# A new hand-stored order of 2278 work pieces in a fused attention and gated-MLP kernel

## Chip, cores, metric

The kernel runs on one core of one Trainium2 chip. The metric is device time in microseconds (us) of one execution, as the median of several runs. Times "in the trace" come from one profiled execution and count from its first instruction.

## What is computed

```python
B, H, S, D = 8, 8, 576, 64
def sm_attn(qq, kk, vv):                       # softmax attention
    s = scale * np.matmul(qq, kk.transpose(0, 1, 3, 2))
    s = s - np.max(s, axis=-1, keepdims=True)
    a = np.exp(s)
    a = a / (np.sum(a, axis=-1, keepdims=True) + 1e-09)
    return np.matmul(a, vv)
...
out_d = sm_attn(q_d, k_d, v_d)                 # q, k, v averaged over 4 positions
out_up = np.repeat(out_d, 4, axis=2)
mask = np.abs(pos[:, None] - pos[None, :]) < 4 # and attention over 7 neighbours
...
x = (out_up + out_local)                       # 8 batches of 576 x 512
h = gelu(x @ w_in)                             # 512 -> 1024, halves u and v
v_n = (v - mu) / np.sqrt(var + 1e-06) * g_ln
v_s = np.einsum('ts,bsd->btd', w_sg, v_n) + b_sg[None, :, None]
return x + (u * v_s) @ w_out
```

## The kernel before, in words

The kernel is written as small **pieces** (`Task`, line 55): a name, the engines that can do it, and a function that emits its instructions. There are 2278. A piece of attention carries the number g = 0 to 31 of its pair of heads (four pairs to a batch), a piece of the MLP the batch and a number, as `s7.1`. The program is the pieces in the order of the string `ORDER` (line 89); `place` (line 66) walks it, gives each piece its buffers from three pools (8 PSUM banks, 10 and 38 SBUF buffers), and the loop at the kernel's end (line 1157 on) emits each piece. A word such as `qs0/V` puts the piece on VectorE; without a letter it goes to the first engine in its table. So the string sets the order on every engine's queue, on the DMA queue of SP, and, where a piece has a choice, its engine. Waits between engines follow from the data; each engine works through its queue strictly in that order.

For each pair g:

- Loads on SP: `lq`, `lk` (q and k), `lv` (v for the pooled attention), `lw` (v in windows). All go through one helper (line 236), which lets at most six be under way.
- `qs`, `ks` (line 481 on DVE as one reduction; lines 484 and 485 on POOL as two additions): sums over four positions, for the pooled scores.
- `S` (L507, L514) local scores and `Y` (L535) pooled scores on PE; from the fifth pair on they are one piece `YS`.
- `mx`, `my` row maxima on DVE; `ea`, `eb`, `ec` exponentials on ACT; `rc`, `np`, `nq` normalization.
- `T`, `U`, `t` (L616, L625) transposes on PE; `pa`, `pb`, `pc`, `pe` (L244) copies out of PSUM.
- `D` (L677, L693): probabilities times v on PE. For the first four pairs `D` reads unsummed v and has four times the pooled matmuls.
- `oe`, `od`, `xa`, `xb` (L700): the pair's x; `xh`, `xl` (L712): x split into two parts for the exact-enough products on PE.

For each batch: `v` (L801; in the first batch cut into `vk` for each pair) and `u` products; `vg`, `vb`, `vp`, `vn`, `vh`, `vl` (L887) the layer norm and its split; `s` (L896) the product over positions; `sa`, `sm` (L943, L949) bias and gate; `ga` to `gd`, `gh`, `gl` (L990, L1002) combinations and splits; `o` (L1019), `oa` (L1026), and the stores `os`. The weights are loaded as 64-bit words and converted on the chip, once, at the start: `wz`, `wy`, `wr` with their `wq`, `wu`, `wb`, `wt`, `wh`, `wl` (L350 to L373), and `wq0` to `wq4` for the square matrix (L441).

At two places (`WARM`) PE gets matmuls on zeros ahead of a piece: 28 ahead of `S0`, 20 ahead of `S3`.

Of the kernel before, what the change touches and what calls it, by code (L numbers as in the profile page):

```python
# [94 lines left out]
wuy3 wqy3/A nq2/P U2 t2 xa0 xb0 ks5/P wby1 xh0/A YS4 pb2/A pc2/A nq3/P np3/P xl0/P t3 lw1 wuy1 wty1 pe2/A whz0/A
wlz0/P ma4 my4 ny4/A mb4 U3 wz2 wqz2/A lv2 ec4 T3 pa3/A pb3/V pc3/A pe3/A D1 mx4 wby3 wty3 lq5 qs5/V wbz2 nx4/A why1/A
wly1/P oe1/A od1 lw3 wuz2 YS5 ma5 vk3.0 xa1 xb1 vk1.0 lv3 ea4 mb5 vk0.0 wtz2 mx5 eb4 whz2/A re4/A my5 ny5/V lw2 nx5/A
D2 why3/A xh1/V ec5 vk2.0 wty2 xl1/V vk3.1 lv4 vs4 D3 wlz2/V rc4 nq4/P wr2 why2/A wly2/P oe2/V od2 xa2 xb2 wq0 wz1 lq6
eb5 ea5 xh2/A wq1 np4/V vk2.1 oe3/V od3 xa3 vk0.1 xb3 xh3/V xl3/P whq0/A U4 xl2/V wly3/V whq1/A wqz1/A t4 re5/A T4
pa4/A vk1.1 pb4/A pc4/A wur2 wbz1 wuz1 xc2 xc0 xc1 vk0.2 wtz1 wqr2/V wbr2 rc5 nq5/P lv5 lk6 np5/P ks6/V pe4/A vk2.2  # L100
v0.2 vg0.2 wq2 wq3 whq3/A wlq3/P vk1.2 v0.0 vg0.0 qs6/V vb0.2/V v0.1 vg0.1 lw4 D4 YS6 whq2/A whz1/A wlz1/P my6 ny6/A
lq8 ma6 mb6 ec6 mx6 nx6/A oe4/V wlq1/V lk7 vs5 wlq0/P vk3.2 od4 xa4 T5 vk4.0 eb6 vk4.1 ks7/V pa5/V vb0.0/V vp0.0 lq7
qs7/V vk4.2 ea6 re6/A u0.4 rc6 qs8/V u0.2 xb4 t5 u0.5 ua0.4 xc3 v0.4 ua0.5 ua0.2 U5 va0.4/A pb5/V pc5/A vb0.1/V u0.3
nq6/P np6/P lk8 v0.3 ks8/V pe5/A lw5 D5 lv6 ua0.3 vp0.2 vg0.3 vn0.0/V b wr1 lw7 wqr1/V vn0.2/A vj0.4 wq4 YS7 oe5/V
vb0.3/A T6 vh0.0/A vg0.4 my7 ny7/A wr0 u0.6 lw6 od5 ma7 mb7 vh0.2/A pa6/V xa5 vp0.1 vn0.1/A ec7 vb0.4/V vh0.1/A ua0.6
u0.1 xb5 mx7 t6 U6 pb6/V pc6/V pe6/V vl0.2/V wlq2/P vs6 u0.0 u0.7 vl0.1/V whq4/A ua0.0 D6 YS8 vp0.3 wur0 ua0.1 nx7/V
vp0.4 vn0.4/V vn0.3/V vh0.4/A ua0.7 wlq4/V ea7 vl0.0/V eb7 vh0.3/V vl0.3/V lv7 vs7 wr3 vl0.4/V s0.1 s0.5 ma8 mb8 re7/A
wbr1 mx8 my8 ny8/A rc7 oe6/A s0.0 ec8 xh5/A nq7/V s0.2 t7 np7/P U7 od6 xa6 sa0.1 sm0.1/P xl5/V sa0.0 wqr0/A lq9 lk9
ks9/V xb6 wur1 wqr3/A lk10 nx8/A T7 s0.3 qs9/V pa7/A pb7/A pc7/A pe7/A lq10 sm0.0/P sa0.2 D7 YS9 eb8 lv8 lk11 qs10/V
sa0.3 sm0.3/V sa0.5 wtr1 ea8 s0.4 sm0.2/P gh0.1/A re8/A vs8 s0.6 xh6/A my9 ny9/A ec9 rc8 np8/V T8 xl6/P oe7/A lw8  # L110
nq8/V U8 sa0.4 ma9 mb9 ks10/V mx9 pa8/A pb8/A pc8/A whr1/A t8 od7 pe8/V sm0.5/P xa7 s0.7 sa0.7 wtr2 ks11/V xh4/A
sm0.4/P sa0.6 xl4/P xb7 xh7/V xl7/P nx9/A eb9 ea9 D8 oe8/A YS10 lq12 v1.1 lv9 gh0.2/A whr2/A ma10 re9/A mb10 xc5 mx10
u1.4 v1.2 xc6 my10 od8 xa8 rc9 xb8 sm0.7/P np9/V T9 gh0.0/A vs9 wlr1/P xc7 v1.0 wbr0 wtr0 ny10/A ua1.4 ec10 vg1.2 wur3
u1.5 nq9/P U9 t9 vg1.0 pa9/A vg1.1 wbr3 wtr3 ua1.5 xc4 gl0.2/V lq11 qs11/V lw9 pb9/A pc9/V v1.3 pe9/V lk12 gl0.0/P
ks12/V vb1.0/A D9 whr0/A YS11 whr3/A lv10 vb1.1/V wlr3/V lw10 vp1.0 nx10/A v1.4 gl0.1/V vn1.0/A vh1.0/A sm0.6/V
gh0.3/A wlr2/V zf3/V my11 vg1.3 vb1.3/A vb1.2/A vp1.2 eb10 gl0.3/V o0.6 ma11 wlr0/V ny11/V vn1.2/A oe9/V mb11 mx11
nx11/A ea11 o0.7 od9 oa0.6 oa0.7 o0.4 oa0.4 vl1.0/P xa9 va1.4/V o0.0 vs10 lk13 qs12/V u1.3 zf0/P vp1.3 vp1.1 oa0.0
ks13/V o0.1 oa0.1 ea10 re10/A rc10 ec11 eb11 o0.3 vj1.4 re11/A vn1.3/A vh1.3/A o0.5 zf1/P zs1/V np10/V rc11 T10 nq11/V
pa10/V oa0.5 vg1.4 o0.2 zs3/V oa0.2 vn1.1/A nq10/V u1.1 vh1.1/V zs2/V U10 pb10/V ua1.1 pc10/A t10 pe10/A xb9 xh8/A
u1.0 ua1.0 vl1.3/V vh1.2/V np11/V vb1.4/A vp1.4 zh2/A zh1/A oa0.3 ua1.3 vn1.4/A D10 oe10/V YS12 my12 lq13 ny12/A ma12  # L120
mb12 ec12 u1.7 vh1.4/A u1.2 od10 os0.2 vl1.1/P xa10 xb10 mx12 ua1.2 lv11 os0.0 nx12/A zf2/P u1.6 vl1.2/P qs13/V U11
vl1.4/V zh3/A T11 pa11/V pb11/A t11 ua1.7 s1.1 sa1.1 os0.3 xh10/A ua1.6 pc11/V pe11/V lw11 ea12 eb12 re12/A s1.0 xl8/V
zs4/V vs11 D11 lv12 YS13 oe11/V s1.2 od11 lk15 sa1.0 my13 vs12 ny13/A lw12 xa11 lq14 qs14/V sm1.0/P ec13 os0.1 s1.4
rc12 nq12/P zl1/V sa1.2 ma13 mb13 mx13 nx13/V s1.3 s1.5 xh9/A xl9/V sm1.2/V np12/V T12 sm1.1/P sa1.3 lk14 sm1.3/P xb11
# [1097 lines left out]
```

## Time and profile before

| | us |
|---|---|
| runs | 564.33, 564.66, 565.92; median 564.66 |
| profiled execution: span from the first to the last instruction | 563.4 |
| median less span | 1.26 |
| PE busy | 547.7 (97%) |
| DVE busy | 445.5 (79%) |
| ACT busy | 392.7 (70%) |
| POOL busy | 331.9 (59%) |
| DMA | 62.73 MB, 111 GB/s on average |

The page states the span of the profiled execution; the time around it is put at the 1.26 us between that span and the median of the runs. PE, DVE, ACT and POOL are the matrix, vector, scalar and GpSimd engines, SP the one whose queue issues the DMAs. "Busy" of PE contains the matmuls on zeros. A matmul's row can start before the one ahead of it has ended, so the length of a row is more than its share of the engine's time.

### The profile page before, as it was taken

How to read it: one execution, taken by the hardware profiler on the slowest of the kernel's cores; microseconds unless marked ns; L12 is line 12 of the kernel's file. 1: busy time of each engine (PE TensorE's matmuls, PEld its weight loads, DVE VectorE, ACT ScalarE, POOL GpSimd, SP SyncE). 2: the span in 40 equal slices, each digit the busy share in tenths (PEclk: the TensorE clock that was granted, in tenths of full speed). 3: DMA queues.
4: the chain of work that ended last, by engine and by line, in shares of the span. 5: the costliest groups of instructions: out<-in, count | busy, mean ns of one | idle time of the engine just before them, and what ended most of it. 6: DMA issues, size and time to landing. Idle time of an engine off the chain costs nothing.

```text
span 563.4 us, 17546 instructions
## 1 busy us (share of the span) xinstructions
PE 547.7 (97%) x6948; PEld 511.2 (91%) x6948; DVE 445.5 (79%) x939; ACT 392.7 (70%) x1320; POOL 331.9 (59%) x447
## 2 busy tenths in 40 slices
...
GB/s 283 273 227 341 203 93 172 95 57 23 181 126 103 34 163 121 100 2 107 153 157 46 46 186 85 136 1 103 92 109 119 66 78 129 71 1 1 0 1 169
DMA packets 31041, 62.73 MB, mean 111 GB/s; under 512 B 3696, under 2 KB 4720, under 8 KB 30960
## 3 DMA queue, kind: packets, MB, share of 16 engines
...
q14 instruction: 26, 0.21, 0.1%
HBM read 52.17 MB, written 9.44 MB: 109 GB/s over the span
## 4 chain that ended last, share of the span: by engine, by line
PE 76%; ACT 6%; DVE 5%; POOL 4%; issue 2%; DMA 0%; DVEq 0%; ACTq 0%; POOLq 0%
PE ps L896 36%; PE ps L801 14%; PE ps L1019 12%; PE ps L677 3%; PE ps L693 2%; PE ps L616 2%; PE ps L625 2%; PE ps L535 2%; PE ps L514 2%; ACT X L574 2%; ACT R L244 1%; DVE R L990 1%; POOL pairs L498 1%; ACT pd L596 1%; POOL wsg_l L441 0%
## 5 line engine op out<-in xcount | busy, mean ns | idle before, releaser
L896 PE MATMUL ps<-wsg_h,R 128*128 128x288 f32 x576 | 122.5, 300 | 0.2 <-DVE R L887 0.2
L896 PE MATMUL ps<-X,weight_z 128*128 128x288 f32 x512 | 109.5, 297 | 0.3 <-ACT R L924 0.3
L801 PE MATMUL ps<-weight_y,X 128*128 128x512 f32 x320 | 98.3, 400 | 0.1
L574 ACT ACTIVATE X<-X,nb 128x64 f32<-128x64 f32 x280 | 93.5, 339 | 5.1 <-DVE nb L553 4.7
L896 PEld LDWEIGHTS ps<-wsg_h,R 128*128 128x128 f32 x576 | 93.9, 188 | 1.3 <-DVE R L887 0.4
L896 PE MATMUL ps<-wsg_l,R 128*128 128x288 f32 x320 | 92.6, 295 | 0.0
L896 PEld LDWEIGHTS ps<-X,weight_z 128*128 128x128 f32 x512 | 84.2, 188 | 1.2 <-ACT R L924 0.6
L896 PE MATMUL ps<-R,weight_z 128*128 128x288 f32 x256 | 75.4, 295 | 0.0
L801 PEld LDWEIGHTS ps<-weight_y,X 128*128 128x128 f32 x320 | 57.6, 188 | 11.9 <-POOL X L244 0.3
L1026 DVE TENSOR_TENSOR R<-ps,R 128x288 f32<-128x288 f32 x98 | 42.1, 448 | 25.2 <-PE ps L1019 24.9
L896 PEld LDWEIGHTS ps<-wsg_l,R 128*128 128x128 f32 x320 | 60.3, 189 | 0.0
L244 ACT COPY R<-ps 128x116 f32<-128x116 f32 (+3 forms) x80 | 27.2, 381 | 40.9 <-DVE R L244 11.9
L574 ACT ACTIVATION_READ_ACCUMULATOR X<-X,nb 128x1 f32 x280 | 53.3, 190 | 0.0
L1019 PE MATMUL ps<-R,weight_r 128*128 128x288 f32 x336 | 51.0, 298 | 0.3 <-DVE R L700 0.3
L244 ACT CAST R<-R 128x576 fp32r<-128x576 f32 (+2 forms) x61 | 39.1, 647 | 17.4 <-POOL R L990 10.5
L801 PE MATMUL ps<-weight_y,R 128*128 128x512 f32 x128 | 50.4, 394 | 0.0
L498 POOL TENSOR_TENSOR pairs<-R 112x256 f32<-112x256 f32 x56 | 45.0, 804 | 6.1 <-DMA R<-in_v_dram 6.0
L896 PEld LDWEIGHTS ps<-R,weight_z 128*128 128x128 f32 x256 | 48.2, 188 | 0.3
L943 DVE SCALAR_TENSOR_TENSOR vs<-ps,g_sb,b_sb 128x288 f32<-128x288 f32 x64 | 32.3, 512 | 20.1 <-PE ps L896 16.9
L1019 PEld LDWEIGHTS ps<-R,weight_r 128*128 128x128 f32 x336 | 46.6, 188 | 1.4 <-issue 0.5
L1002 POOL TENSOR_TENSOR R<-R,R 128x576 fp32r<-128x576 f32 x21 | 32.1, 1534 | 23.4 <-ACT R L244 9.8
L949 POOL TENSOR_TENSOR R<-R,vs 128x288 f32<-128x288 f32 x27 | 24.5, 909 | 35.4 <-DVE vs L943 29.4
...
## 6 DMA issues: line engine op xcount, KB each, us to landing
...
X<-in_vw_dram SPq DMA_DIRECT2D x32, 320.0 KB, 4.4
R<-in_kT_dram SPq DMA_DIRECT2D x32, 293.0 KB, 3.9
R<-in_qT_dram SPq DMA_DIRECT2D x32, 293.0 KB, 3.8
...
weight_z<-in_w_in_dram SPq DMA_DIRECT2D x4, 512.0 KB, 5.8
weight_y<-in_w_in_dram SPq DMA_DIRECT2D x4, 512.0 KB, 6.0
weight_r<-in_w_out_dram SPq DMA_DIRECT2D x4, 512.0 KB, 5.8
```

What stands on the lines that cost most here:

```text
L244: (nc.scalar.copy if e == "A" else ENG[e].tensor_copy)(**kw)
L498: ENG[e].tensor_tensor(out=pairs, in0=v[:, 0:2], in1=v[:, 2:4], op=ALU.add)
L514: nc.tensor.matmul(out=sp[i][os, c * KB:(c + 1) * KB], lhsT=q[hs, t * QB:t * QB + KB], rhs=k[hs, t * QB:t * QB + KB], start=not early, sto ...
L574: nc.scalar.activation(out=st["ms"][:, t, :], in_=src, func=AF.Exp, bias=st["nb"][:, t:t + 1], scale=scale, accum_out=sums[par][:, t:t + 1])
L677: nc.tensor.matmul(out=out, lhsT=lhsT, rhs=pdt[ks, probs, h * QC:(h + 1) * QC], start=first, stop=last)
L801: nc.tensor.matmul(out=acc, lhsT=r32(l), rhs=r32(weights[f"y{k}"][:, 0, w]), start=(i == 0 and ks[0] == 0), stop=(i == len(ops) - 1 and ks ...
L896: nc.tensor.matmul(out=acc[:, 0:HALF], lhsT=r32(l), rhs=r32(r), start=(first and n == 0), stop=(last and n == len(ops) - 1))
L943: nc.vector.scalar_tensor_tensor(out=vsb[i], in0=at["ps", "m", b, "s", i][:, 0:HALF], scalar=g_sb[:, i // 2:i // 2 + 1], in1=b_sb[:, half( ...
L949: ENG[e].tensor_tensor(out=gate(i), in0=gate(i), in1=vsb[i], op=ALU.mult)
L1002: ENG[e].tensor_tensor(out=r32(gl[m]), in0=us[raws[m]], in1=gh[m], op=ALU.subtract)
L1019: nc.tensor.matmul(out=bank(j, c), lhsT=r32(l), rhs=r32(r), start=first and i == 0, stop=i == len(ops) - 1, skip_group_check=not first)
L1026: nc.vector.tensor_tensor(out=x, in0=bank(j, c), in1=x, op=ALU.add)
```

## The change

Only the string `ORDER` is another; the pieces, their functions, the pools and everything else are the same. Of the string's 2278 words nearly all stand at another place, and 369 pieces go to another engine: for instance 25 of the 40 `vl` are on POOL where 17 were, and 32 of the 40 `vb` on ACT where 25 were. The first lines of the table:

```diff
 ORDER = """
-wz3 wuz3 lk0 ks0/P wqz3/V wbz3 wy0 wqy0/V wby0 lq0 lk2 lk1 wtz3 whz3/A wlz3/P S0 lq1 qs0/V Y0 mx0 ia0 lq3 my0 ks1/P
-wuy0 qs1/P ib0 ea0 small wty0 S1 mx1 ks2/V lq2 qs2/P ia1 es0 ny0/A ec0 re0/A ib1 ea1 Y1 lk3 my1 rc0 S2 mx2 why0/A ia2
...
+wz3 wqz3/V wuz3 lq0 qs0/P wbz3 wtz3 whz3 lk0 ks0 S0 lk1 ks1 mx0 lq2 Y0 wy0 wqy0 qs2/P wlz3 lq1 my0 S1 ia0 ny0/V ib0 wby0
+qs1/P lk5 lk2 wuy0 mx1 wty0 ea0 es0 ec0 re0 ia1 lq3 why0 Y1 qs3/P my1 rc0 nq0 wy2 wqy2 wuy2 lk3 wz0 ny1 S2 S3 mx2 ib1
...
```

Three places are shown as the built programs have them. In the rows of the change every line number below the table is smaller by 10, since its table is ten lines shorter.

The first loads in SP's queue, before (`weight_z3`, `weight_y0` are `wz3`, `wy0`; the `R` buffers are `lk0`, `lq0`, `lk2`, `lk1`, `lq1`):

```order
L236 DMA weight_z3_154<-in_w_in_dram 128x2x512
L236 DMA R0_157<-in_kT_dram 128x586
L236 DMA weight_y0_167<-in_w_in_dram 128x1024
L236 DMA R3_174<-in_qT_dram 128x586
L236 DMA R4_176<-in_kT_dram 128x586
L236 DMA R5_178<-in_kT_dram 128x586
L236 DMA R6_237<-in_qT_dram 128x586
```

And in the change (`wz3`, `lq0`, `lk0`, `lk1`, `lq2`, `wy0`, `lq1`):

```order
L226 DMA weight_z3_154<-in_w_in_dram 128x2x512
L226 DMA R0_158<-in_qT_dram 128x586
L226 DMA R2_170<-in_kT_dram 128x586
L226 DMA R3_226<-in_kT_dram 128x586
L226 DMA R4_231<-in_qT_dram 128x586
L226 DMA weight_y0_243<-in_w_in_dram 128x1024
L226 DMA R5_250<-in_qT_dram 128x586
```

The load of `weight_y0` moved from the third place to the sixth, so q and k of the first pair are now second and third.

DVE's queue from the first weight to the first row maximum, before (L352 to L358 convert a weight; L481 is `qs0`; L544 is `mx0`):

```order
L352 TENSOR_SCALAR weight_z3_154<-weight_z3_154 128x512
L308 MEMSET mask_sb_70 128x3
L309 MEMSET mask_sb_70 128x7
L356 TENSOR_SCALAR ps0_163<-weight_z3_154 128x512
L358 SCALAR_TENSOR_TENSOR R1_164<-weight_z3_154,ps0_163 128x512
L352 TENSOR_SCALAR weight_y0_167<-weight_y0_167 128x512
L356 TENSOR_SCALAR ps1_170<-weight_y0_167 128x512
L358 SCALAR_TENSOR_TENSOR R2_171<-weight_y0_167,ps1_170 128x512
L481 TENSOR_REDUCE qd0_80<-R3_174 128x144
L544 TENSOR_REDUCE stats0_84<-ps2_213 128x4
```

And in the change (L471 twice: `ks0`, `ks1`; L534: `mx0`):

```order
L342 TENSOR_SCALAR weight_z3_154<-weight_z3_154 128x512
L298 MEMSET mask_sb_70 128x3
L299 MEMSET mask_sb_70 128x7
L346 TENSOR_SCALAR ps0_163<-weight_z3_154 128x512
L348 SCALAR_TENSOR_TENSOR R1_164<-weight_z3_154,ps0_163 128x512
L471 TENSOR_REDUCE kd0_88<-R2_170 128x144
L471 TENSOR_REDUCE kd1_89<-R3_226 128x144
L534 TENSOR_REDUCE stats0_84<-ps1_202 128x4
```

The three operations on `weight_y0` went behind the first row maximum (one of them to ACT); `qs0` went to POOL, and `ks0`, `ks1` came from POOL to DVE.

POOL's queue in the last batch, around the splits `vl` that the product `s7.1` waits for, before (L887 is `vl7.3`; L853 to L855 are `vp`; L1002 is `gl6.5`):

```order
L854 TENSOR_TENSOR rs_104<-rs_104,nhalf 128x1
L855 TENSOR_SCALAR nm_109<-mv_101,rs_104 128x1
L887 TENSOR_TENSOR R_8486<-R_8440,R_8483 128x512
L853 TENSOR_SCALAR rs_105<-rs_105 64x1
L854 TENSOR_TENSOR rs_105<-rs_105,nhalf 64x1
L855 TENSOR_SCALAR nm_110<-mv_102,rs_105 64x1
L1002 TENSOR_TENSOR R_8550<-R_7730,R_8548 128x576
```

And in the change (L877 is `vl`: `vl7.4`, then `vl7.1`, `vl7.0`, `vl7.3`; L992 is `gl6.4`, and last `gl6.6`):

```order
L992 TENSOR_TENSOR R_8481<-R_8320,R_8322 128x576
L877 TENSOR_TENSOR R_8483<-R_8369,R_8483 64x512
L843 TENSOR_SCALAR rs_104<-rs_104 128x1
L844 TENSOR_TENSOR rs_104<-rs_104,nhalf 128x1
L845 TENSOR_SCALAR nm_109<-mv_101,rs_104 128x1
L877 TENSOR_TENSOR R_8525<-R_8371,R_8465 128x512
L877 TENSOR_TENSOR R_8539<-R_8277,R_8520 128x512
L877 TENSOR_TENSOR R_8580<-R_8487,R_8535 128x512
L992 TENSOR_TENSOR R_8621<-R_8405,R_8619 128x576
```

Before, one of the batch's five `vl` was on POOL and four on DVE; now four are on POOL, three of them in a row.

## Rows read from the trace of the kernel before

**Rows 1.** Stretch, length, busy PE, PEld, DVE, ACT, POOL; PE clock, DMA share, GB/s.
```profile
0.00:70.50 70.50, 59.43 (x1078) 49.86 (x1079) 60.66 (x142) 53.09 (x182) 55.55 (x72) 0.95 0.82 265
14.10:28.20 14.10, 12.36 (x237) 10.51 (x232) 13.94 (x32) 11.91 (x44) 12.26 (x15) 0.86 0.86 273
70.50:549.90 479.40, 477.97 (x5796) 451.21 (x5795) 377.01 (x781) 338.60 (x1138) 272.96 (x375) 1.00 0.28 87
549.90:563.40 13.50, 10.33 (x79) 10.10 (x77) 7.81 (x19) 1.01 (x2) 3.41 (x2) 1.00 0.49 176
```

**Rows 2.** What PE waited for: us in total, times, longest.
```profile
PE ps L514 <- DMA R<-in_qT_dram: 2.3, 1, 2.3
PE ps L693 <- issue: 2.2, 1, 2.2
PE ps L535 <- DVE qd L481: 2.1, 2, 1.4
```

**Rows 3.** Timeline of PE: start us, length us, line, operation [idle before <-releaser].
```profile
8.68 0.93 PE L514 MATMUL ps<-R,R 64*64 64x64 f32 x40 [2.30 <-DMA R<-in_qT_dram]
11.00 1.18 PE L535 MATMUL ps<-kd,qd 64*64 64x144 f32 x16 [1.38 <-DVE qd L481]
...
25.51 2.93 PE L677 MATMUL ps<-R,R 48*64 48x144 f32 x56
...
33.47 1.72 PE L677 MATMUL ps<-R,R 48*64 48x144 f32 x59
...
41.10 1.71 PE L677 MATMUL ps<-R,R 48*64 48x144 f32 x60
...
45.06 1.71 PE L677 MATMUL ps<-R,R 48*64 48x144 f32 x60
...
49.47 0.45 PE L693 MATMUL ps<-R,X 64*64 64x58 f32 x13 [2.19 <-issue]
...
57.42 0.63 PE L677 MATMUL ps<-R,vd 48*64 48x144 f32 x15
```

**Rows 4.** Timeline of DVE in the first 22 us.
```profile
5.16 0.43 DVE L352 TENSOR_SCALAR weight_z<-weight_z 128x512 f32<-128x512 f32 x1 [1.80 <-DMA weight_z<-in_w_in_dram]
...
6.35 0.69 DVE L358 SCALAR_TENSOR_TENSOR R<-weight_z,ps 128x512 int32<-128x512 int32 x1
7.68 1.06 DVE L352 TENSOR_SCALAR weight_y<-weight_y 128x512 f32<-128x512 f32 x1 [0.64 <-DMA weight_y<-in_w_in_dram]
...
10.10 0.75 DVE L481 TENSOR_REDUCE qd<-R 128x144 f32<-128x576 f32 x1
10.77 0.88 DVE L544 TENSOR_REDUCE stats<-ps 128x4 f32<-128x256 f32 x2
...
21.62 0.88 DVE L544 TENSOR_REDUCE stats<-ps 128x4 f32<-128x256 f32 x2
```

**Rows 5.** DMA issues by kind, from the page: count, size of one, median us to landing.
```profile
R<-in_v_dram SPq DMA_DIRECT2D x16, 96.0 KB, 5.4
X<-in_vw_dram SPq DMA_DIRECT2D x32, 320.0 KB, 4.4
R<-in_kT_dram SPq DMA_DIRECT2D x32, 293.0 KB, 3.9
weight_y<-in_w_in_dram SPq DMA_DIRECT2D x4, 512.0 KB, 6.0
```

**Rows 6.** The chain that ended last, two unbroken runs on PE: start us, us.
```profile
38.89 2.27 PE ps L801 x9
...
547.55 12.70 PE ps L1019 x96
```

**Rows 7.** Busy time by stretch, two microseconds of the first `D`; columns as in rows 1.
```profile
26.00:28.00 2.00, 2.00 (x49) 2.00 (x45) 1.98 (x5) 1.99 (x8) 2.00 (x2) 0.50 0.53 147
```

**Rows 8.** Line 887 (`vl`) by engine: duration ns min/median/max, first and last start us.
```profile
L887 DVE TENSOR_TENSOR R<-R,R x23: 673/686/1659, 79.2 to 526.5; 128x512 fp32r<-128x512 f32 x16, 64x512 fp32r<-64x512 f32 x7
L887 POOL TENSOR_TENSOR R<-R,R x17: 1267/1295/1355, 128.2 to 519.6; 128x512 fp32r<-128x512 f32 x16, 64x512 fp32r<-64x512 f32 x1
```

More of the change, by code (lines that the diff above doesn't have):

```diff
@@ L89 @@
 ORDER = """
-wz3 wuz3 lk0 ks0/P wqz3/V wbz3 wy0 wqy0/V wby0 lq0 lk2 lk1 wtz3 whz3/A wlz3/P S0 lq1 qs0/V Y0 mx0 ia0 lq3 my0 ks1/P
-wuy0 qs1/P ib0 ea0 small wty0 S1 mx1 ks2/V lq2 qs2/P ia1 es0 ny0/A ec0 re0/A ib1 ea1 Y1 lk3 my1 rc0 S2 mx2 why0/A ia2
-es1 ib2 qs3/P ny1/A Y2 my2 np0/P ec1 re1/A rc1 ea2 es2 nq0/P S3 mx3 ia3 wy2 wuy2 lv0 T0 pa0/A wz0 ks3/P wqz0/V ib3
-wuz0 lk4 t0 U0 ny2/A ec2 np1/P pb0/A wbz0 pc0/A lk5 nq1/P t1 U1 re2/A T1 pa1/A ea3 wqy2/A lq4 rc2 ks4/V pe0/A Y3 my3
-ny3/A wly0/P qs4/P lw0 es3 wy1 wqy1/A ec3 pb1/A pc1/A wtz0 wby2 pe1/A lv1 D0 oe0/V od0 np2/P T2 re3/A rc3 pa2/A wy3
@@ L95 @@
[L95 to L124, printed above, removed]
@@ L205 @@
-oa7.16 os7.3.1 o7.03 os7.1.1 o7.02 oa7.04 os7.0.0 gl7.6/P o7.14 oa7.06 os7.0.1 oa7.13 os7.3.0 o7.04 oa7.03 os7.2.0
+wz3 wqz3/V wuz3 lq0 qs0/P wbz3 wtz3 whz3 lk0 ks0 S0 lk1 ks1 mx0 lq2 Y0 wy0 wqy0 qs2/P wlz3 lq1 my0 S1 ia0 ny0/V ib0 wby0
+qs1/P lk5 lk2 wuy0 mx1 wty0 ea0 es0 ec0 re0 ia1 lq3 why0 Y1 qs3/P my1 rc0 nq0 wy2 wqy2 wuy2 lk3 wz0 ny1 S2 S3 mx2 ib1
+np0 T0 ia2 mx3 ea1 ec1 pa0 es1 wqz0 ks2 U0 pb0 ib2 re1 ks3/P Y3 wuz0 ia3 lw0 rc1 lv0 wz2 lq4 ib3 wly0 Y2 pc0 t0 my2 pe0
+wbz0 my3 ea2 D0 es2 ks5/P nq1 ea3 lk4 ks4 np1 T1 lq5 ny2 ec2 oe0 od0 pa1 ny3 U1 lw1 pb1 re2 rc2 es3 t1 ec3 pc1 wuz2 re3
@@ new lines @@
+wy1 wuy1 wby2 wqy1 wtz0 qs4/P YS4 rc3 xa0 wy3 my4 pe1 wqz2 xb0 nq2 np2 U2 ny4 T2 pa2 ma4 np3 wby1 t2 ec4 nq3 xh0 wty2
+pb2 T3 pa3 pc2 pe2 mb4 wty1 U3 pb3 pc3 mx4 lv1 qs5 why1 wbz2 D1 oe1 lw2 lv2 YS5 wqy3 wuy3 D2 xl0/P wtz2 whz0/V wlz0
+nx4/V eb4 od1 xa1 ma5 mb5 xb1 wby3 wly1 t3 pe3 xh1/V ea4 wz1 wqz1 my5 ny5/V re4/V rc4 vk2.0 vk0.0 wty3 xl1 oe2 why2 wuz1
+od2 nq4 xa2 lv3 lw3 ec5 lk6 D3 oe3/V wq1 whq1 lv4 xb2 xh2 vs4 lq7 wly2 mx5 wq0 lq6 od3 xa3 np4/V nx5 eb5 vk0.1 t4 xb3
+vk2.1 vk3.0 vk3.1 ks6 vk1.0 xl2 T4 pa4 why3 xh3/V U4 wbz1 vk1.1 pb4/V ea5 re5/V wr2 lw4 rc5 wqr2 wly3 wq3 wq2 whq2 pc4/V
@@ new lines @@
+wlr2 o0.0 oa0.0 ea10 qs13 re10/V vs10 o0.2 ks12 zf3 o0.3 vh1.0 rc10 vh1.1 ea11 oa0.2 oa0.6 zf1/V ks13/P xb9 eb11 xh8/V
+ny11 ec11 re11 lq12 o0.1 oa0.1 os0.0 o0.5 rc11 va1.4 nq10/V vp1.3 u1.1 zs1 vj1.4 np11 vg1.4 o0.7 vb1.4 np10 T10 oa0.3
+nq11/V U10 oa0.7 os0.3 ua1.0 vl1.1 pa10 pb10/V oa0.5 pc10 t10 u1.3 pe10 vp1.4 ua1.1 ua1.3 qs12 D10 YS12 vn1.2 vh1.2
+vl1.2/P zf0/V os0.1 vl1.0 ma12 mb12 vn1.3/A T11 pa11/V vh1.3 vl1.3/P u1.2 vn1.4/A vh1.4/V vl1.4/P ua1.2 oe10 od10 zf2
+lw11 U11 pb11 lq14 lv11 my12 t11 ny12/V xa10 xb10 mx12 vs11 u1.6 ua1.6 qs14 u1.7 zs3/V zs2/V xh9 ua1.7 s1.0 sa1.0 lw12
```

172 lines of the change are left out of this document (92 added, 80 removed).

## The prediction

> **What bounds the kernel now.** First the table of busy time by stretch [rows 1]. The reader is to see two different programs in it. From 70.5 to 549.9 us PE is busy 477.97 of 479.40 us: 1.43 us of idle time in 85% of the span, while DVE has 102 us to spare, ACT 141 and POOL 206. Before 70.5 us PE is idle for 70.50 - 59.43 = 11.07 us, and after 549.9 for 3.17. So PE is the bound, its work is the same in both orders, and an order can win only what PE loses at the start, at most some 11 us of 15.7. Second, the list of what PE waited for [rows 2]: the loads of q for 2.3 us, sums on DVE for 2.1, and 2.2 us with no wait that the profile can name. Third, the timelines of PE and DVE [rows 3, 4], which show how the first pieces hang together. DVE is busy 13.94 of the 14.10 us from 14.1 to 28.2 [rows 1], so there the start is DVE's as much as PE's. I argue from when certain pieces start, and above all `D4` at 57.42 [rows 3]: in both orders the 43 pieces ahead of `D4` in PE's queue are the same set, so a microsecond by which `D4` starts sooner is a microsecond won, if nothing gives it back later.
>
> **The start, step by step.** *Loads.* From 5.16 us, when DVE can use the first weight, to 8.68, when `S0` can use q, three loads land: 293 + 512 + 293 KB [rows 3 to 5]. That is 1098 KB in 3.52 us, 312 KB a microsecond. The change puts q and k of the first pair second and third. They land at 5.16 + 293/312 = 6.1 and 7.04, so `S0` starts at 7.1 in place of 8.68.
>
> *`Y0`.* Before, it waited until 11.00 for `qs0`, which stood on DVE behind the three operations on `weight_y0` (7.68 to 10.10) [rows 3, 4]. Now `ks0` stands on DVE straight behind the first weight, whose last operation ends at 6.35 + 0.69 = 7.04, and `qs0` on POOL, which has q a microsecond sooner. `ks0` takes 0.75 (the same reduction as `qs0`), so `Y0` starts at 7.9, 3.1 us sooner. `mx0` follows `ks0` and `ks1` on DVE: 7.1 + 2 x 0.75 = 8.6 in place of 10.77. What was in front of it is not gone: `weight_y0` now comes between `ib0` and `mx1`, on a queue with no idle time, so only part of these microseconds lasts.
>
> *`mx3`.* `S3` needs the load `lk3`, now the eleventh after the first weight: nine of 293 KB and two of 512, 3661 KB, landing at 5.16 + 11.7 = 16.9. That is later than the compute would ask for, and it is where a queue pays for loads that went ahead (`lk5`, `wy2`). With 0.93 for `S3`, `mx3` starts at 17.9 in place of 21.62. The six DVE pieces that now stand behind it (`es1`, `ks2`, `ib2` and others) follow at once.
>
> *`D0`.* Its last input is the copy `pe0`, behind `t0`, behind `Y2`, which waits for `ks2`, two places behind `mx3`: 17.9 + 0.88 + 0.8 (`es1`) + 0.75 (`ks2`) + 0.8 for `Y2` and 0.4 for transpose and copy, 21.5. Its loads `lw0` and `lv0` (320 KB and four of 96 [rows 5]) are in by 5.16 + 4877/312 = 20.8. Before, its large block began at 25.51 [rows 3]. It ran 2.93 us, where the blocks of the next three take 1.72; the granted clock was 0.50 then [rows 7], the 1.2 GHz level. In the change PE waits less ahead of it; whether the clock is higher is open, worth 0 to 1.2 us, and I count 0.
>
> *`D1` to `D3`.* `D1` needs `lv1`: 12 x 293 + 6 x 512 + 2 x 320 + 8 x 96 = 7996 KB behind the first weight. By 312 KB/us that is 30.8, by the 273 of the stretch from 14.1 [rows 1] it is 34.4. I take 32.1, nearer the first, because that stretch's queue itself had waits for compute. Before it was 33.47. `D2` follows with only `YS5` between (2.5 for `D1`, 1.2 for `YS5`): 35.8. `D3` comes after `D2`, a transpose and two of the `vk` pieces (three matmuls each, 2.27 / 3 = 0.76 [rows 6]): 35.8 + 2.5 + 0.2 + 1.5 = 40.0, with 0.4 for a late `lw3`, 40.4. Before: 41.10 and 45.06 [rows 3].
>
> *`D4`.* 40.4 + 2.5 for `D3`, twelve `vk` and `v` pieces of 0.76, and 0.9 for `T4`, `U4`, `t4`: 52.9. I add 0.5 for hand-overs and take 53.4, against 57.42: **4.0 us sooner**. Condition: ACT must deliver the copies and `xh2`, `xh3` between 30 and 50 us in step; it was busy 53.09 of the first 70.50 us [rows 1], so it can, but not with much to spare.
>
> *The unnamed wait.* Of the old way from `D3` to `D4`, 2.19 us are the stop at 49.47 inside `D3` [rows 3], for which no semaphore answers. The 4.0 holds it as gone. If it comes back whole, 1.8 is left. It is tied to nothing in the order that I can see; I put it at a third, 0.7.
>
> **Behind the start.** The middle has 1.43 us of idle time to win; a denser use of POOL could cost more. Eight more of the `vl` go to POOL, where one takes 1.295 us in place of 0.686 [rows 8]. The nearest case is the last batch: four on POOL, three of them in a row, 3 x 1.3 = 3.9 us. Their cover is what PE has between `v7.3` and `s7.1`: five `o` pieces of 12.70 / 16 = 0.79 [rows 6] and three `u` pieces of twice that, 8.7 us. The layer norm of `v7.3` on ACT and POOL takes some 3 us ahead of them, so 1.8 us are left over: cost 0. On DVE one of these splits took 1.659 us [rows 8], 0.97 over its median: it met something on POOL, and the median of 0.686 beside the shortest of 0.673 says that this is rare. The Trainium skill (SBUF — State Buffer, Who interferes with whom) says that a VectorE instruction with two SBUF inputs and a GpSimd instruction that reads SBUF exclude each other for the whole instruction. By that rule each of the eight could hold up DVE for a full 1.295 us, 10.4 us in all, in place of 0.97 now and then. Either goes into DVE's 102 idle microseconds, so by both the sum stays, and what it would cost without cover is the second rival.
>
> The tail: after the last `s` thirteen `o` pieces (10.3 us) run before `o7.03` needs `gl7.2`, the fifth of a chain on POOL of about 1.46 each (1.295 x 576/512), 7.3 us and 1.0 for bias and gate: covered by 2. After the last `o` the same addition and store follow. 0.
>
> **Sum.** 563.4 - 4.0 + 0.7 = 560.1 us of span, and 1.26 around it, as in the median of the runs: **561.4 us**, against 564.66 (-0.6%). About 0.3% (1.7 us) is what a measurement of this kernel can tell from no change, so faster begins under 563.0 and slower above 566.4.
>
> **Rivals.** *1. The start gives its lead back: 563.8.* If the stop of 2.19 us returns and `D1` waits for its loads until 34.4 (2.3 later, half of it made up because PE has `vk` pieces to do meanwhile), 4.0 - 2.2 - 1.1 = 0.7 is left. For it: DMA was busy 0.82 of the first 70.5 us [rows 1], and the change consumes faster. Against it: it takes both.
>
> *2. POOL becomes late: 571.2.* The place is the split ahead of `s` in batches 0, 3, 4, 6, 7, where POOL gets the eight more `vl`: 8 x (1.295 - 0.686) = 4.9 us, and one collision of 0.97 in each of five batches, 4.9, together 561.4 + 9.8. It decides once POOL ends more than 1.8 us later than worked out for the last batch. For it: POOL's queue is strict, a late `vp` holds all `vl` behind it. Against it: 206 us of idle time, and four batches with three `vl` on POOL before, without a wait in the list. By the rule of the Trainium skill named above (SBUF — State Buffer, Who interferes with whom) a collision would be 1.295 and this case 572.8; no row shows one that long.
>
> *3. All goes well: 559.0.* The stop is gone, no term is made smaller, the middle loses its 1.43 and the first `D` runs at the higher clock for half of its 1.2: 561.4 - 0.7 - 1.1 - 0.6.
>
> That the change does not do what it says has no room: PE's queue has as many rows in both programs, and the number of activation-table loads on ACT is 48 in both.
>
> **How the numbers follow.** Forecast 0.50 (560.0 to 562.9), rival 3 0.15, rival 1 0.21, rival 2 and other losses 0.14. Faster 0.65, same 0.21, slower 0.14. The range goes from the lower end of rival 3 with all of the clock's 1.2 counted and a microsecond more from the loads, 557.6, to 565.8, past rival 1; it leaves rival 2 out.
>
> **What would show it.** Right: in the new profile `S0`'s q-k matmuls start at 7.1 and `Y0` at 7.9, the second `D` before 33.5, `D4` near 53.4 (the first matmuls on `vd`), idle time of PE before 70.5 us about 7 us, and about 1.5 in the middle. Wrong: `D4` at 56 or later, with PE waiting for `vw` or v loads or for ACT's copies between 30 and 50 us; or over 4 us of idle PE after 70 us, with releasers on POOL (`vl`, `gl`) ahead of L896 or L1019.

## Result and profile after

The changed kernel takes **570.13 us** (median of 20 runs, 566.37 to 573.44) against 564.90 for the kernel before in the same session (20 runs): ratio 1.0080, 95% interval 1.0060 to 1.0101. The forecast was 561.4, faster, with a range up to 565.8. It is slower by 0.8%.

The profiled execution took 568.25 us, its span 566.4. First the busy time by stretch, with the columns of [rows 1]:

```profile
0.00:70.50 70.50, 58.65 (x1077) 49.13 (x1078) 61.10 (x144) 52.78 (x179) 53.19 (x71) 0.98 0.81 265
14.10:28.20 14.10, 11.72 (x277) 9.90 (x276) 13.26 (x33) 12.02 (x42) 13.36 (x18) 1.00 0.85 286
70.50:549.90 479.40, 475.84 (x5781) 449.05 (x5780) 365.52 (x749) 342.65 (x1148) 317.49 (x415) 1.00 0.29 88
549.90:566.40 16.50, 12.81 (x95) 12.34 (x93) 9.98 (x21) 1.35 (x2) 7.57 (x5) 1.00 0.30 108
```

PE loses 11.85 us before 70.5 us, where it lost 11.07, and 3.56 us in the middle, where it lost 1.43. So the start has won nothing and the middle has lost 2.1. POOL has 45 us more to do in the middle and still a third of it idle. What PE waited for, in us (total, times, longest):

```profile
PE ps L606 <- ACT R L234: 2.0, 1, 2.0
PE ps L525 <- issue: 1.8, 1, 1.8
PE ps L886 <- issue: 1.7, 1, 1.7
PE ps L683 <- issue: 1.6, 1, 1.6
PE ps L525 <- ACT pd L586: 1.5, 1, 1.5
PE ps L504 <- DMA R<-in_qT_dram: 1.5, 1, 1.5
...
PE ps L886 <- DVE R L877: 0.7, 2, 0.3
```

The reader should see the word "issue" three times. In [rows 2] it stood once, with 2.2 us: a stop for which no semaphore answers. Now there are three of 1.6 to 1.8 us, 5.05 in all. Two are in the start, and PE's timeline, read against [rows 3], shows where (`...` stands for rows left out):

```profile
7.51 0.75 PE L504 MATMUL ps<-R,R 64*64 64x64 f32 x34
8.06 0.34 PE L525 MATMUL ps<-kd,qd 64*64 64x144 f32 x2
...
21.30 1.74 PE L667 MATMUL ps<-R,R 48*64 48x144 f32 x58 [0.21 <-issue]
...
31.61 0.71 PE L606 MATMUL ps<-turn_l,X 122*128 122x122 f32 x5 [2.05 <-ACT R L234]
32.55 1.69 PE L667 MATMUL ps<-R,R 48*64 48x144 f32 x58
...
37.22 0.29 PE L525 MATMUL ps<-kd,qd 64*64 64x96 f32 x1 [1.80 <-issue]
...
38.29 2.89 PE L667 MATMUL ps<-R,R 48*64 48x144 f32 x56
...
43.77 1.71 PE L667 MATMUL ps<-R,R 48*64 48x144 f32 x60
...
47.68 0.33 PE L683 MATMUL ps<-R,X 64*64 64x58 f32 x4 [1.57 <-issue]
...
58.72 0.64 PE L667 MATMUL ps<-R,vd 48*64 48x144 f32 x15
```

`D0` (21.30) starts 4.2 us sooner than before and its large block takes 1.74 us, 2.93 before. `D1` (32.55) comes 0.9 sooner. Then the lead goes: a stop ahead of `D2` (38.29), `D2` itself at the price that `D0` paid before (2.89), a stop in `D3` (43.77), and `D4` at 58.72, 1.3 us later than before. The slow block is the clock, by the busy time of two-microsecond stretches:

```profile
36.00:38.00 2.00, 0.78 (x34) 0.78 (x38) 1.46 (x3) 1.85 (x9) 2.00 (x3) 0.87 0.46 143
38.00:40.00 2.00, 2.00 (x51) 2.00 (x47) 1.52 (x4) 0.78 (x6) 1.08 (x1) 0.50 0.87 224
40.00:42.00 2.00, 2.00 (x81) 1.99 (x73) 1.97 (x5) 0.00 (x0) 0.81 (x1) 0.77 0.82 272
```

PE stood still for 1.2 of the 2 us from 36 to 38, and behind that the granted clock is 0.50, the 1.2 GHz level. This stop was paid twice; behind the other two the clock stayed at 1.00.

The third stop lies in the middle of `u4.0`, between two matmuls of one product whose operands had long been there:

```profile
335.60 0.42 PE L886 MATMUL ps<-X,weight_z 128*128 128x288 f32 x2
337.70 0.29 PE L886 MATMUL ps<-R,weight_z 128*128 128x288 f32 x1 [1.68 <-issue]
```

The profile has one clue. Among the DMA queues it lists 55 transfers of the kind "instruction" with 0.90 MB, 16 KB each: one for every 126 of the 6948 matmuls with their weight loads. By size and number these are fetches of PE's own program: 0.90 MB over twice 6948 instructions is 65 bytes for one, and with 128 matmuls more (`g4` below) there are 56 of them. The Trainium skill (Trainium Architecture — The Big Picture, The software stack) gives an instruction 64 bytes. The DMA view of the stretch from 314 to 335 us (queue and kind: packets, MB, share), first of the kernel before, then of the change:

```profile
q1 hardware_dynamic: 1106, 2.27, 37.4%
q8 instruction: 2, 0.03, 0.6%
q14 instruction: 1, 0.01, 0.1%
```

```profile
q1 hardware_dynamic: 1023, 2.06, 31.5%
q14 instruction: 1, 0.01, 0.1%
```

Two fetches on queue 8 before, none in the change; the next one came at 335.45 us, when nine loads and stores had filled DMA since 329. The count by itself says little, since it depends on where a fetch falls in the window. The times say more: the 16 KB were in at 336.42, and PE went on at 337.70, 1.28 us later. The two stops in the start end 1.21 and 1.41 us behind such a transfer (in at 36.01 and 46.27), and that of the kernel before 1.28 us (in at 48.19, PE on at 49.47). In the twenty profiles of this document PE has 31 stops of 1 us or more without a releaser; 29 of them end 1.2 to 1.7 us after a fetch was in, while fetches come 4 to 11 us apart in the start. So PE ran on what it had, and stood until the next piece of its program was there.

### The profile page after: what moved, and what is told of

Same layout as the page of the kernel before. It is cut to its first block, busy times and chain, and to the rows that moved or that the text cites. A ratio compares the mean times of both kernels' runs of the same rounds, so it can differ in the third digit from the quotient of the medians.

```text
span 566.4 us, 17587 instructions
## 1 busy us (share of the span) xinstructions
PE 547.3 (97%) x6948; PEld 510.5 (90%) x6948; DVE 436.6 (77%) x912; ACT 396.8 (70%) x1328; POOL 378.2 (67%) x490
## 3 DMA queue, kind: packets, MB, share of 16 engines
q1 hardware_dynamic: 30960, 61.62, 34.4%
## 4 chain that ended last, share of the span: by engine, by line
PE 82%; DMA 9%; DVE 5%; POOL 1%; issue 1%; SPq 0%; ACT 0%; DVEq 0%; POOLq 0%
PE ps L886 39%; PE ps L791 15%; PE ps L1009 14%; DMA weight_z<-in_w_in_dram 4%; PE ps L606 3%; PE ps L667 3%; PE ps L683 2%; PE ps L504 2%; PE ps L615 2%; PE ps L525 2%; DMA R<-in_qT_dram 2%; DMA weight_y<-in_w_in_dram 1%; DMA X<-in_vw_dram 1%; DMA R<-in_v_dram 1%; DVE R L690 1%
## 5 line engine op out<-in xcount | busy, mean ns | idle before, releaser
L791 PE MATMUL ps<-weight_y,X 128*128 128x512 f32 x320 | 97.0, 397 | 0.0
L234 ACT COPY R<-ps 112x192 f32<-112x192 f32 (+4 forms) x83 | 29.4, 392 | 32.8 <-PE ps L606 14.7
L933 DVE SCALAR_TENSOR_TENSOR vs<-ps,g_sb,b_sb 128x288 f32<-128x288 f32 x64 | 32.4, 512 | 21.5 <-PE ps L886 18.0
L992 POOL TENSOR_TENSOR R<-R,R 128x576 fp32r<-128x576 f32 x24 | 37.6, 1571 | 14.3 <-ACT R L234 9.2
L877 POOL TENSOR_TENSOR R<-R,R 128x512 fp32r<-128x512 f32 (+1 forms) x25 | 33.3, 1342 | 19.2 <-DVE R L234 8.9
```

The costliest lines, as they stand in the source:

```text
L234: (nc.scalar.copy if e == "A" else ENG[e].tensor_copy)(**kw)
L791: nc.tensor.matmul(out=acc, lhsT=r32(l), rhs=r32(weights[f"y{k}"][:, 0, w]), start=(i == 0 and ks[0] == 0), stop=(i == len(ops) - 1 and ks ...
L877: ENG[e].tensor_tensor(out=r32(dst), in0=vact[s][0][0:n], in1=vh[0:n, 0:DM], op=ALU.subtract)
L933: nc.vector.scalar_tensor_tensor(out=vsb[i], in0=at["ps", "m", b, "s", i][:, 0:HALF], scalar=g_sb[:, i // 2:i // 2 + 1], in1=b_sb[:, half( ...
L992: ENG[e].tensor_tensor(out=r32(gl[m]), in0=us[raws[m]], in1=gh[m], op=ALU.subtract)
```

## Experiments

Theories: **A** the loss lies in the order behind the start; **B** the start leaves something behind that slows all that follows; **D** PE's stops are late fetches of its instructions, so they depend on where a fetch falls and what DMA does then. The rival of the prediction is a late POOL. Of the long lines of `ORDER` the diffs below show only the words around a change.

**Half and half.** `e1` has the changed order up to `YS7` (the same 59 pieces of PE in both), the old one behind it; `e2` is the mirror. At the seam of `e1`:

```diff
-ua0.5 np6/V D5 lv6 YS7 wqr1/V oe5/V od5 xa5 my7 ua0.3 xb5
+ua0.5 np6/V D5 lv6 YS7 small wur2 qs8 nq6 ks8/V ua0.3 b
```

> The changed order up to and including YS7 (the first 70 us), the order of before behind it, each piece with the engine that it has in its own half. Theory A (the loss lies behind the start, the start itself is worth nothing, since YS7 ran at 72.61 us in the changed kernel and at 72.72 before): 564 to 566 us, and D4 again late, near 58 us. Theory B (the start leaves something behind that slows all that follows, a lower granted clock for instance): 568 to 571 us, and the granted clock of most runs under 0.993. What the prediction said of the start (4 us sooner): 561 us.

> The mirror of the kernel above: the order of before up to and including YS7, the changed order and its engines behind it. Theory A: 568 to 570 us, with 1.5 us lost between YS7 and v1.0 and some 2 us at one stop inside u4.0. Theory B: 564 to 566 us, with the granted clocks of before. If the two halves only cost where they come together, both kernels give about 565.

`e1` took 566.00 us, ratio 0.9999 (0.9976 to 1.0023); `e2` 569.40, ratio 1.0050 (1.0028 to 1.0072). So A: in the median the new start, with its seam, is worth nothing, and the new rest costs some 0.5%, 2.8 us. That this is less than the change's 0.8% lies within the two intervals. One part of the expectation missed: in `e1`'s profile `D4` stands at 56.97, not near 58. That execution, 2 us under its median, reached `YS7` 1.9 us sooner than the profile before, and gave 0.7 back behind the seam (491.4 us from `YS7` to the end, 490.7 before). In `e2`'s trace the longest wait behind 70 us is again the one inside `u4.0`, now 2.5 us and put down to an instruction of ACT that produces nothing `u4.0` reads; that name is a coincidence of times: a fetch was in at 338.66, and PE went on at 340.12, 1.46 us later.

**Order and engines apart.** `e3` has the new order with the old engines (its first words are shown), `e4` the old order with the new engines:

```diff
-wz3 wqz3/V wuz3 lq0 qs0/P wbz3 wtz3 whz3 lk0 ks0
+wz3 wqz3/V wuz3 lq0 qs0/V wbz3 wtz3 whz3 lk0 ks0/P
```

> The changed order of all 2278 pieces, each on the engine that it has in the kernel before (369 pieces go back, 93 of them from POOL to DVE, 67 from DVE to POOL). If the engines are the loss (the second rival, a late POOL), about 565 us; if the order is, as in the changed kernel, 568 to 571. An order that was searched for other engines may also be worse than both, over 571: then it tells nothing of the engines.

> The order of before with the engines of the change. If the engines are the loss: 568 to 571 us with waits on POOL behind 70 us; if the order is: 564 to 566. Above 571 it tells nothing, as in the kernel above.

641.94 us (ratio 1.1343) and 659.34 (1.1647). Both far above 571, so by their own terms they say nothing of POOL. They show that here an order and its engines belong together.

**Fewer transfers under way.**

```diff
-DEPTH = 6
+DEPTH = 3
```

> The changed kernel with at most three transfers under way in place of six (DEPTH 3). Theory D: the stops of PE that have no semaphore are late fetches of its own instructions, which wait behind the transfers that are queued; with half as many queued a fetch comes some 2.8 us sooner (three transfers of 0.94 us), the stop of 1.68 us inside u4.0 goes, and those of 1.80 and 1.57 us in the start with it: 3 to 5 us less than the changed kernel, 565 to 567 us. Rival: the stops have another cause, the first 58 us are bound by the loads, and fewer of them under way make them slower: 570 to 575 us with the stop inside u4.0 as before.

> The kernel before with the same DEPTH 3. Theory D: the stop of 2.19 us inside the fourth D goes, 562 to 564 us. Rival: slower loads in the start, 567 to 572 us.

579.56 (1.0253) and 576.08 us (1.0193): both times on the rivals' side, since the loads of the start were slower with three under way (`YS7` at 85.55 and 81.36 us in the profiles, 72.61 and 72.72 with six). Yet the stops went, as D had it: `f1` has no wait of PE listed between 330 and 360 us, so that in `u4.0` is gone, and its longest without a releaser is 0.6 us; `f2` has none at all, where the kernel before had 2.19. `f1`'s first waits show what replaced the gain:

```profile
PE ps L525 <- DVE kd L471: 4.5, 2, 3.9
PE ps L504 <- DMA R<-in_qT_dram: 3.3, 1, 3.3
PE ps L606 <- ACT R L234: 2.9, 1, 2.9
```

**Making room for the fetch.** In the change SP waits 11.4 us for the additions that the store `os3.3` needs, while DMA is idle, and then issues everything at once. `f3` puts four loads ahead of that store:

```diff
-o3.12 oa3.02 oa3.14 oa3.13 os3.3 o3.13 oa3.16 o3.04
+o3.12 oa3.02 oa3.14 oa3.13 lw23 lq24 lk25 lk24 os3.3 o3.13 oa3.16 o3.04
...
-oa3.04 np22 lw23 lq24 vp4.3 lv22
+oa3.04 np22 vp4.3 lv22
...
-xa21 ma23 lk25 ec23 vs22
+xa21 ma23 ec23 vs22
...
-u4.4 eb23 lk24 ks24/P vn4.3
+u4.4 eb23 ks24/P vn4.3
```

> The changed kernel with four loads (lw23, lq24, lk25, lk24) issued ahead of the store os3.3, for which SP waits 11.4 us while DMA is idle; nothing else moves. Theory D: the nine transfers that fill DMA from 329 to 337 us become five, the fetch finds room, the stop of 1.7 us inside u4.0 goes: 567.5 to 568.5 us in the runs where the changed kernel has 570. Rival: the stop belongs to the place in the program or to the operands of u4.0 and stays: 570 us.

566.43 us, ratio 1.0030 (1.0009 to 1.0051): by the ratios 0.5%, 2.8 us, under the change, more than expected. The stretches of its trace (columns as in [rows 1]) show DMA done by 332 us, and PE with hardly a gap:

```profile
330.00:332.00 2.00, 2.00 (x78) 1.64 (x80) 1.84 (x4) 1.05 (x1) 1.79 (x4) 1.00 0.95 343
332.00:334.00 2.00, 2.00 (x59) 1.93 (x53) 1.67 (x6) 1.88 (x7) 1.33 (x3) 1.00 0.06 17
334.00:336.00 2.00, 1.96 (x15) 1.86 (x15) 1.93 (x5) 1.97 (x6) 0.99 (x3) 1.00 0.03 8
```

**Moving the fetches.** `f4` leaves the order as it is and only changes how many instructions stand ahead of `S0`, where PE waits for q anyway. The matmuls are on zeros and nobody reads them; in either form they keep PE busy for 5 to 6 us, by the execution (to 7.05 us in the change's profile, 5.80 in `f3`'s, 6.09 in this one, 6.91 in that of `m1`, the same kernel).

```diff
-WARM = {"S0": 28, "S3": 20}
+WARM = {"S0": 12, "S3": 20}
...
                 for _ in range(WARM[t.name]):
                     nc.tensor.matmul(out=spare[:, 0:2 * P], lhsT=zeros[:, 0:P], rhs=zeros, start=True, stop=True)
+                for _ in range(64 if t.name == "S0" else 0):
+                    nc.tensor.matmul(out=spare[:, 0:KB], lhsT=zeros[:, 0:P], rhs=zeros[:, 0:KB], start=True, stop=True)
```

> The changed kernel with 12 wide and 64 narrow zero matmuls ahead of S0 in place of 28 wide ones: PE is busy as long (6 us), but every later instruction stands 48 matmuls further on in PE's program, so that its fetches fall at other pieces. Theory D: the stop inside u4.0 goes or moves, and those of the start move too; 567 to 570 us. Rival (the stop belongs to u4.0 itself): it stays at the same matmul and the time is 570.

**564.47 us**, ratio 0.9995 (0.9973 to 1.0017), below the expected range: by this alone the loss against the kernel before is gone. PE has no wait listed between 300 and 350 us, and the DMA view from 314 to 335 has two fetches:

```profile
q1 hardware_dynamic: 1354, 2.74, 40.7%
q8 instruction: 2, 0.03, 0.6%
q14 instruction: 1, 0.01, 0.2%
```

**Is it the place, or the narrow matmuls?** `g4` shifts by 128 matmuls, one whole fetch; `g2` gives the old order the shift of `f4`; `g3` joins `f3` and `f4`; `g1` joins `e1` and `f4`.

```diff
-WARM = {"S0": 28, "S3": 20}
+WARM = {"S0": 1, "S3": 20}
...
+                for _ in range(155 if t.name == "S0" else 0):
+                    nc.tensor.matmul(out=spare[:, 0:KB], lhsT=zeros[:, 0:P], rhs=zeros[:, 0:KB], start=True, stop=True)
```

> The changed kernel with 1 wide and 155 narrow zero matmuls ahead of S0, 128 more than the 28 of the changed kernel, for the same 6 us. A fetch holds 16384 bytes, and 55 of them cover 6948 matmuls with their weight loads, 126 pairs each; so 128 pairs are one whole fetch, and every piece stands at the same place within a fetch as in the changed kernel. Theory D: the stops come back, the one inside u4.0 among them: 569 to 571 us. If narrow matmuls in place of wide ones made the gain: 564 to 565 us.

> The kernel before with the same 12 wide and 64 narrow zero matmuls. Theory D says only that its stop of 2.19 us inside the fourth D may go or move, since its fetches fall elsewhere: 562.5 to 565.5 us. If the narrow matmuls themselves made the gain of the shifted kernel (5.6 us), by keeping TensorE in another state, this kernel gains as much: 559 to 560 us.

> Both mends of the changed kernel at once: four loads ahead of the store os3.3, and the shifted fetches. Theory D: at u4.0 they mend the same stop, so it is won once; 563.5 to 565 us, as with the shift alone. If they were two separate gains (3.7 and 5.7 us) they add up: 561 us.

> The changed order up to YS7, the order of before behind it, and the zero matmuls of the run with shifted fetches (12 wide, 64 narrow). If the start was only zero because of its late fetches and the rest of the changed order loses some 1.5 us by its waits, this takes the better half of each: 562 to 563 us, under both kernels. Rival (the start is worth nothing with any fetches): 565 to 566.

`g4`: 571.14 us, ratio 1.0106 (1.0068 to 1.0143). With 155 narrow matmuls the time is that of the change, so it is the place within a fetch. The stop is back, in the same matmul of `u4.0`, and the stretches behind it show its second price as well:

```profile
341.19 0.29 PE L886 MATMUL ps<-R,weight_z 128*128 128x288 f32 x1 [2.16 <-issue]
```

```profile
340.00:342.00 2.00, 0.81 (x7) 0.81 (x7) 1.86 (x5) 1.97 (x13) 0.99 (x3) 1.00 0.10 36
342.00:344.00 2.00, 2.00 (x12) 2.00 (x11) 0.44 (x1) 2.00 (x14) 1.87 (x2) 0.59 0.03 8
344.00:346.00 2.00, 2.00 (x11) 2.00 (x10) 1.47 (x4) 1.51 (x7) 1.76 (x4) 0.56 0.00 0
346.00:348.00 2.00, 2.00 (x18) 2.00 (x17) 1.97 (x4) 1.97 (x3) 2.00 (x2) 1.00 0.00 0
```

PE is "busy" all the time from 342 to 346, yet does 12 and 11 matmuls in 2 us where it does 18 after. The clock's share lost there is 2 x (1 - 0.59) + 2 x (1 - 0.56) = 1.7 us, beside 2.2 for the stop.

`g2`: 563.53 us, ratio 0.9967 (0.9946 to 0.9988), not the 5.6 us less that narrow matmuls would have had to bring. `g3`: 565.22, ratio 1.0003, 0.2 us above its range: the two mends do not add up, as they should not if they mend the same stop. `g1`: 566.12, ratio 0.9996 (0.9969 to 1.0023), a miss: not under both kernels.

**What was still open.** Does the depth of the queue matter behind the start, and does any offset set the start free?

```diff
+        deep = DEPTH if len(moves) < 61 else 3
-        if len(moves) >= DEPTH:
+        if len(moves) >= deep:
```

> The changed kernel with six transfers under way for the first 61 (all ahead of YS7) and three for the rest. Theory D: the loads of the start are as fast as in the changed kernel, and the stop inside u4.0 goes, because a fetch waits for three transfers in place of six: 566 to 567 us, as with the four loads moved ahead of the store. Rival (the depth of the queue has nothing to do with it, only the time at which DMA is full): the stop stays and the time is 570 to 572.

> The changed kernel with 22 wide and 30 narrow zero matmuls ahead of S0: 24 more than the 28, for the same 6 us. Theory D: the time depends on the offset alone and lies between that at 48 (564.5 us) and at 0 or 128 (570 to 571); if the u4.0 stop is gone, 564 to 567.

> The changed kernel with 8 wide and 108 narrow zero matmuls: 88 more than the 28. Theory D: 564 to 571 us, by where the fetches of the start and of u4.0 fall; an offset at which neither meets a full DMA would give D4 at 55 us or earlier, and 562 us. If only offsets near 48 help, about 570.

> The changed order up to YS7, the order of before behind it, at offset 24. The start is that of k2; the rest has no stop at u4.0 at any offset tried. Theory: 563 to 566 us, under k2 by the waits of the changed rest (0.5 to 1 us) and by the u4.0 stop if k2 has it.

`k1`: 567.22 us, ratio 1.0047 (1.0025 to 1.0068). The stop is there in the same matmul, but 0.26 us long, though DMA is busy 0.75 to 0.96 from 330 to 338:

```profile
337.22 0.29 PE L887 MATMUL ps<-R,weight_z 128*128 128x288 f32 x1 [0.26 <-issue]
```

The change, `f1`, `f3` and `k1` have one program on PE, so that one fetch, the 35th, can be followed through them: it begins when PE has begun 4410 matmuls in `f1`, 4478 in `f3`, 4504 in `k1` and 4515 in the change. The stop in `u4.0` is none, none, 0.26 and 1.68 us. The later the same piece of the program comes, the longer PE stands.

`k2` 567.33 (1.0037) and `k4` 566.19 (1.0024), both just above their ranges, and `k3` 565.85 (1.0017): none has a wait at `u4.0`, and none frees the start. `k3`'s profile stops for 4.65 us inside `D0`, from 24.7 to 29.3 us, and has a granted clock of 0.70, 0.50 and 0.52 in the three stretches of 4 us from 26 on; its `YS7` starts at 76.77. No offset brought `D4` below 56.68 (`f4`).

**The two orders at one offset.** `m1` is `f4` and `m2` is `g2` once more, on one chip:

> The changed order at offset 48 once more, beside the old order at the same offset. If the late fetches are the whole of the loss, the two orders are equal within 1 us, near 564 us.

> The old order at offset 48. Under the kernel before by 1 to 2 us again (its stop inside the fourth D falls elsewhere, but another took its place in the profile); if it is under the changed order by over 1.5 us, the changed order loses by its waits as well.

`m1` 565.02 us, ratio 0.9998 (0.9977 to 1.0019); `m2` **563.11**, ratio 0.9968 (0.9943 to 0.9993). The old order with shifted fetches beats both kernels, twice by the same 0.3%. And at equal offset the changed order is 0.3% (1.7 us) behind the old one, as `f4` is behind `g2`; not within the 1 us that late fetches alone would have left. In the profiles 1.4 us of it lie behind `YS7` (492.2 us from there to the end in `m1`, 490.7 in `m2`): it has waits of its own.

## Why the prediction was wrong

**The start up to `D1` came out, in part by luck.** `S0`'s q-k matmuls 7.1 (measured 7.51), `Y0` 7.9 (8.06), `mx3` 17.9 (17.57), `D0` 21.5 (21.30), `D1` 32.1 (32.55). `Y0` and the chain from `mx3` to `D0` went as worked out. But the loads were faster at first than the 312 KB/us of the sum: q and k of the first pair were in by 6.71, and `lk3` at 14.89, not 16.9 (some 380 KB/us). `S0` and `S3` stood behind something that the prediction left out, the matmuls on zeros ahead of them, which ended at 7.05 and 16.43. `D1`'s own loads were in by 31.75, within 30.8 to 34.4; what it stood behind is the longest wait of the list, 2.05 us for a copy of ACT, which had itself waited 1.52 us for the load of `weight_y`, until 28.95, and had weights to convert before the copy.

**The step that failed is the unnamed wait:** "It is tied to nothing in the order that I can see; I put it at a third, 0.7." It was taken for an accident of one execution that might return once, and came to 5.05 us in three stops, with 1.2 for the clock behind one. It is a late fetch of PE's program, and comes in the start of every variant with six transfers under way, at places that move with the offset and with lengths that differ between executions of one kernel: 1.14 and 1.50 us in `f4`, 0.46, 0.80 and 0.39 in `m1`. From `D1` on: `D2` 38.05 for 35.8 (the stop of 1.80), `D3` 43.77 for 40.4 (the clock at 0.50 in `D2`: 2.89 - 1.71 = 1.2), `D4` 58.72 for 53.4 (the stop of 1.57, and 0.9 for a result of POOL inside `v0.2`). The four sum to 5.5 us; `D4` missed by 5.3. The prediction's own sign of being wrong had `D4` at 56 or later, but with loads or ACT's copies as the cause. The clock had been seen for `D0` [rows 7], and counted as something that might get better; it moved to `D2`.

In the eleven profiles with the new start, six transfers under way and a mean granted clock above 0.98, the first matmul of `YS7` lies between 70.6 and 76.8 us; in the four with the old start at 72.7, 74.6, 71.9 and 71.4. Both means are 72.65. That the start is worth nothing in the mean is shown by this and by `e1`. That it would be worth its 4 us without late fetches is not: no run with six transfers had a start without them.

**The middle was taken as safe** ("1.43 us of idle time to win"), and that was the costlier error: 3.1 of the 6.3 us between 560.1 and 566.4 of span arise behind `YS7` (493.8 us from there to the end, 490.7 before). About 1.8 are the stop in `u4.0`, a kind of loss that the prediction had only in the start. In the medians it is worth 2.8 us (`f3` against the change). That the clock falls behind it in many executions, as in `g4`'s profile, would account for the difference, though the runs give only a mean clock: of the 20 runs, the nine with a mean granted clock of 0.994 or more took 566.4 to 570.2 us, the eleven below it 569.8 to 573.4. The profiled execution, at 0.997, was one of the cheap ones, and its 568.25 lies below the median.

**Rival 2** (POOL late, 571.2) had the number by chance, since most of the loss is another, but a part of its mechanism took place. POOL was not late: no wait of PE behind 70 us names it. What happened is the collision. The prediction priced it at 0.97 us, or 1.295 at most, and let it go into DVE's idle time. Two of them, in time with what PE waited for behind each:

```profile
79.79 1.78 DVE L857 TENSOR_SCALAR R<-R,mv,rs 128x512 f32<-128x512 f32 x1
79.98 1.30 POOL L877 TENSOR_TENSOR R<-R,R 128x512 fp32r<-128x512 f32 x1
82.08 0.58 PE L667 MATMUL ps<-R,vd 48*64 48x144 f32 x14 [0.59 <-DVE R L234]
...
552.61 4.72 POOL L992 TENSOR_TENSOR R<-R,R 128x576 fp32r<-128x576 f32 x3
552.87 1.80 DVE L992 TENSOR_TENSOR R<-R,R 128x576 fp32r<-128x576 f32 x1
554.72 0.53 PE L1009 MATMUL ps<-R,R 128*128 128x288 f32 x2 [0.52 <-DVE R L992]
```

`vl0.2`, one of the eight that went to POOL, runs within an instruction of the layer norm on DVE (L857), and that takes 1.78 us where its median is 0.54, so 1.24 more, nearer the 1.295 than the 0.97; it takes 1.75 to 1.80 beside `vl0.2` in every profile with the new rest. DVE had no idle time there: it has hardly a break from 78.5 to 88 us, so all that follows on it comes later, the copy for `D6` (0.6 us of PE) and the two splits on DVE for the first `s` products (0.7, at 86 and 87 us). In the last batch a split on DVE takes 1.80 us beside one on POOL, median 0.76 (0.5 of PE). That DVE's instructions were long because of POOL's is read from these traces; no run moved `vl0.2` back by itself. Line 877 by engine, to be read against [rows 8]:

```profile
L877 POOL TENSOR_TENSOR R<-R,R x25: 1268/1303/1837, 80.0 to 528.9; 128x512 fp32r<-128x512 f32 x20, 64x512 fp32r<-64x512 f32 x5
...
L877 DVE TENSOR_TENSOR R<-R,R x15: 672/682/1852, 75.6 to 528.9; 128x512 fp32r<-128x512 f32 x12, 64x512 fp32r<-64x512 f32 x3
```

The longest of these on DVE is 1.17 us over its median. At the good offset the listed waits behind 70 us come to 2.1 us in `m1`, 1.7 of them the three above, against 1.5 of other kinds in `m2`: part of the 1.7 us by which the new order trails; the rest is not accounted for. **Rival 1** (the start gives its lead back, 563.8) named what happened in the start, with the returning stop in it, and stopped there. Its terms add up to 564.0, and rival 3's, with the whole 1.43 us of the middle, to 558.7; neither slip bears on the outcome.

**The tail** was right from the end of PE's last matmul to the end, 3.2 us in both, but not ahead of it: the 0.5 us in the last products had been put at 0.

**What stays open.** When PE asks for a fetch no row shows, only when it comes. That it then waits behind the queued transfers fits `f1`, `f3` and `k1`, where the same fetch comes sooner with fewer of them, and would explain why three queued transfers leave 0.26 us of 1.7. But the Trainium skill (DMA: Bandwidth & Descriptors, Queues, rings and completion order) says that a DMA engine goes round its queues packet by packet, and by that a fetch on a queue of its own would wait for a packet, not for six transfers. The runs show a dependence on the transfers; by which way they hold the fetch up they don't show.
